# A decode layer's last attention head: four-at-a-time rows of the output projection, another cut of the last V piece, paired output rows

## The chip, the cores and the metric

The kernel runs on one core of one Trainium2 chip. The metric is device time in microseconds (us) of one execution, the median of several. Engines are named as in the profile: PE (TensorE, matrix products), PEld (its weight loads), DVE (VectorE), ACT (ScalarE), POOL (GpSimd) and SP (SyncE, which here only issues transfers). Some transfers can also be issued by ACT.

## The reference

One token passes a layer: layer norm, attention over a cache, projection, residual; then layer norm, a gated feed-forward block, residual.

```
q = (layernorm(x) @ wq)            # 32 query heads of 128, from 512
scores = q . k * 128**-0.5         # 8 key/value heads, 4 query heads share one; 65536 positions
o = softmax(scores) @ v
h = x + o @ wo                     # wo: 4096 x 512
g, u = layernorm(h) @ w_gate, layernorm(h) @ w_up     # 512 x 1792 each
out = h + (sigmoid(g) * u) @ w_down                   # 1792 x 512
```

All inputs are bf16. K and V are 8 x 65536 x 128 each, 268 MB together; with the weights 282 MB are read.

## The kernel before, in words

**Tiles and stages.** The 65536 positions of a head are cut into 32 chunks (`TC` = 16 positions on each of 128 partitions, 512 KB a chunk), and each of K and V comes in two pieces of 16 chunks (`PIECES`), 8 MB each. The pieces go through the buffer `ring`. For each head, DVE transposes K chunk by chunk into `ktw`, PE multiplies by the query (scores into four PSUM banks), the maximum is taken, ACT makes the exponentials, DVE transposes them into `PT_sb`, and PE multiplies V by them (PV). PV goes in *rounds* of two chunks: eight products, on four column groups of the PE array, accumulated in PSUM bank 4 (`PO`). 16 rounds make a head: eight for the first piece, eight for the second.

**What sets the order.** Each engine has its own list of operations; `Prog` puts semaphore waits between them. SP issues all transfers but x in one order (`load`, lines 322 to 360), some behind a wait for a buffer to come free. PE's list for the heads is a loop over code written once, with branches by registers (`pe_flow`, lines 674 to 758). A head has four *parts*, told apart by the register `w`: scores of a quarter of the keys, and in the second and fourth part eight PV rounds of the head before. The eight rounds run as 6 + 2 (registers `m` and `k`), with a detour through `waits` between. A ninth pass of the loop (`i == i_last`) has no scores; it does the PV of head 7 in its second and fourth part, and passes the first and the third empty.

**The last head.** Its second V piece (V7.1) comes as two transfers, 12 chunks and 4 chunks (`LAST`). Ahead of them SP issues w_o as two transfers, the 28 rows that belong to heads 0 to 6 and the last four (`WO`); behind them w_gate, w_up and w_down (`WD_SPLIT`: 8, 4 and 2 of its 14 rows). While V7.1 is under way, PE does section L, which is `project7` and `columns`: `regroup(0)` (L620, L626, L629) puts the outputs of 28 query heads in order in `O3`; 28 products of one column of `O3` with 512 columns of w_o add up one row in PSUM bank 5 (L645, the loop through L430, L663); DVE copies the row to `yr` (L665); four fp32 products turn it into four columns (L671). Then section V3 waits for V7.1's first piece, six PV rounds follow, section VL waits for the second, two rounds follow.

**Behind the last round**: ACT scales and copies the sums (L604), PE adds up and ACT copies them (L607, L610), `regroup(1)` and `project` add the last four query heads (L620, L626, L629, L636, 16 products), layer norm (L807, L388 to L402), gate and up (L821: 32 products of 448 columns, four column groups), the gate's function (L828, L829), the product `hh` (L831), its transpose `hhT` (L834), 56 products with w_down on four column groups, each giving one PSUM row (L839), a copy of four rows of 128 into `y_sb` (L845 on DVE, L847 on ACT, two each), and one transfer out from SP (L849).

L430 is a helper (`mm_at`) through which all products with addresses in registers pass: scores, PV and the w_o rows have that one line.

Of the kernel before, what the change touches and what calls it, by code (L numbers as in the profile page):

```python
# [215 lines left out]
def bass_sequential_preLN__gqa_block_cached__glu_gated_glu__decode_kernel(  # L216
# [18 lines left out]
    RW = 4  # L235
    WD_SPLIT = [(0, 8), (8, 12), (12, 14)]
    FG = FF // 4

    with ExitStack() as es:
        def sb(name, shape, dt):  # L240
            return es.enter_context(nc.sbuf_tensor(name, shape, dt))
# [19 lines left out]
        qz = sb("qz", [128, 8 * 64], bf16)  # L261
        yr = sb("yr", [1, 512], fp32)
        po_sb = sb("po_sb", [128, 512], bf16)
# [29 lines left out]
        hh = sb("hh", [128, FG], bf16)  # L293
        hhT = sb("hhT", [128, FG], bf16)
        y_sb = sb("y_sb", [1, D], bf16)

# [21 lines left out]
        W_AT = {"wg": AT["wg"] * CH, "wu": AT["wg"] * CH + 4 * FF}  # L318
        LAST = [(16, 28), (28, 32)]

# [23 lines left out]
        load("V", h, 0, [f"F{h}.1"], "va", f"V{h}.0")  # L344
        for i, (j0, nj) in enumerate(WO):
            src = A_wo[j0 * DH:(j0 + nj) * DH, :].rearrange("(p r) n -> p (r n)", r=nj)
            dst = ktw[:, j0 * D:(j0 + nj) * D]
            dma("sp", lambda e, src=src, dst=dst: e.dma_start(dst, src), f"wo{i}", [f"PV{h - 1}.3"] if i == 0 else (), f"wo{i}")
        for i, cols in enumerate(LAST):
            load("V", h, 1, (), ("vb", "vl")[i], f"V{h}.1{('', 'b')[i]}", cols)  # L350
        for k, w in (("wg", B_w_gate), ("wu", B_w_up)):
            src = w.rearrange("(p k) n -> p (k n)", p=128)
            for i, (k0, k1) in enumerate(W_SPLIT[k]):
                at = W_AT[k]
                dma("sp", lambda e, at=at, w=src, a=k0 * FF, z=k1 * FF: e.dma_start(ring[:, at + a:at + z], w[:, a:z]),
                    f"{k}{i}", [f"PV{HKV - 1}.1"] if k == "wg" else (), f"{k}.{i}")
# [8 lines left out]
        for nm, t, v in (("onesf", onesf[:, :], 1.0), ("xz0", xz[:, :], 0.0), ("onef", one_f[:, :], 1.0), ("nhalf", nhalf[:, :], -0.5),  # L365
                         ("gs0", gsel[:, :], 0.0), ("zcol", zcol[:, :], 0.0), ("qh0", qh[:, :], 0.0), ("qz0", qz[:, :], 0.0),
                         ("PTz", PT_sb[:, 4 * 512:PT_ROW], 0.0), ("Wz", ktw[:, W0:KTW_ROW], 0.0)):
            op("pool", lambda e, t=t, v=v: e.memset(t, v), name=nm)
# [10 lines left out]
        op("dve", lambda e: e.tensor_reduce(blk_of[:, :], identf[:, :].rearrange("p (c r) -> p c r", r=RW), AX.X, ALU.max), (), "blk")  # L379
        op("dve", lambda e: e.tensor_reduce(bass.AP(tensor=gsel, offset=0, ap=[[128, 128], [32, 4]]),  # L380
                                            identf[:, :].rearrange("p (s j) -> p s j", s=4), AX.X, ALU.add), ["gs0", "identf"], "gsel")

# [87 lines left out]
        op("act", lambda e: e.activation(ps(1, 0, 512, 0, 8), bass.AP(tensor=zcol, offset=0, ap=[[1, 8], [0, 512]]), AF.Copy), ["zcol"], "zq")  # L470
        op("pe", project_q, ["zq", "xz", "wq", "identf", "lsel", "onef", "sel", "gsel", "row", "PTz", "qz0"], "q")
        op("act", lambda e: e.activation(  # L472
# [118 lines left out]
        def pv(h, r, rounds):  # L591
            P.part["pe"] = ("B", (h, r, rounds))
            name = f"PV{h}.{r}" + "a" * (rounds == 6)
            for k in range(2):
# [45 lines left out]
        def project7():  # L640
            regroup(0)
            waits = ["O3.0", "wo0"]
            def rows(e):
                out = ps(YB, 0, D, 0, 1)
                e.matmul(out, lhsT=O3[:, 0:1], rhs=ktw[:, 0:D], start=True, stop=False, skip_group_check=True)  # L645
                ra, ro, rb, rp, left = (reg(e, i) for i in range(16, 21))
                n = NQ - GS
                e.reg_mov(ra, addr_of(ktw, D))
                e.reg_mov(ro, addr_of(O3, 1))
                e.reg_mov(left, n // 2 - 1)  # L650
                e.reg_alu(rb, ra, 2 * D, ALU.add)
                e.reg_alu(rp, ro, 2, ALU.add)
                goto("rows")
                for x, y in ((ra, ro), (rb, rp)):
                    mm_at(e, out, at_reg(O3, y, [[NQ, 128], [1, 1]]), at_reg(ktw, x, [[KTW_ROW, 128], [1, D]]), False, 32)
                for x in (ra, rb):
                    e.reg_alu(x, x, 4 * D, ALU.add)
                for x in (ro, rp):
                    e.reg_alu(x, x, 4, ALU.add)
                e.reg_alu(left, left, -1, ALU.add)  # L660
                e.br_ne(left, 0, on_true="rows", on_false="rows_end")
                label("rows_end")
                return e.matmul(out, lhsT=O3[:, n - 1:n], rhs=ktw[:, (n - 1) * D:n * D], start=False, stop=True, skip_group_check=True)  # L663
            op("pe", rows, waits, "yr")
            op("dve", lambda e: e.tensor_copy(yr[:, :], ps(YB, 0, D, 0, 1)), ["yr"], "yrs")  # L665

        def columns():

            for nt in range(4):
                lhsT = bass.AP(tensor=yr, offset=nt, ap=[[D, 1], [4, 128]])  # L670
                op("pe", lambda e, lhsT=lhsT, nt=nt: e.matmul(ps(YT, nt, nt + 1), lhsT=lhsT, rhs=one_f[0:1, 0:1], start=(nt == 0),  # L671
                                                              stop=False, skip_group_check=True), ["yrs"] if nt == 0 else ())
        def pe_flow(e, section):
# [6 lines left out]

            i, w, p, v, m, k, s = (R.setdefault(n, e.alloc_register(f"r_{n}")) for n in "iwpvmks")
            w0, p0 = addr_of(ktw, W0 + NC - 1 + 127), addr_of(PT_sb, 31 * 4)
# [6 lines left out]
            e.reg_mov(i, i_first)  # L689
            e.reg_mov(s, step[0])  # L690
            goto("head")
            e.reg_mov(w, w0)
# [23 lines left out]
            label("values3")  # L716
            away("br_eq", i, i_last, "rows_of_o", lambda: section("L"))
            e.reg_mov(v, v_at)
# [26 lines left out]
            goto("next", "part")  # L745
            e.reg_alu(w, w, -4, ALU.add)
            e.br_ne(w, w0 - 16, on_true="part", on_false="head_end")
            label("head_end")
            e.br_eq(i, i_last, on_true="after", on_false="more_heads")
            label("more_heads")  # L750
            section("X")
            e.reg_alu(i, i, -lag, ALU.add)
            nc.br("head", engines=here)
            for name, body, back, under in later:
                label(name, under)
                body()
                nc.br(back, engines=here)
            label("after", "head_end")

# [10 lines left out]
        for i in range(HKV + 1):  # L770
            loop, last = 0 < i < HKV, i == HKV
            for r in range(NR):
# [12 lines left out]
                if i and r == 3:  # L785
# [5 lines left out]
                    op("pe", lambda e: None, [f"V{i - 1}.1"])  # L791
                    pv(i - 1, r, 6)
                    if last:
                        P.part["pe"] = ("VL", i)
                        op("pe", lambda e: None, [f"V{i - 1}.1b"])
                    pv(i - 1, r, 2)
                    P.part["pe"] = ("O", i)
# [18 lines left out]
        for i, (nm, bank) in enumerate((("wg", GB), ("wu", UB))):  # L816
            at = W_AT[nm]
            for kt in range(4):
                for c in range(4):
# [13 lines left out]
                                            sg2[:, :].rearrange("p (q r) -> p r q", r=NF), ALU.mult), ["gu1", "sg2"], "hh")  # L833
        op("dve", lambda e: e.transpose(hhT[:, :], hh[:, :]), ["hh"], "hhT")  # L834
        for i, (r0, r1) in enumerate(WD_SPLIT):
            for r in range(r0, r1):
                for g in range(4):
                    last = r == NF - 1 and g == 3
                    op("pe", lambda e, r=r, g=g: e.matmul(  # L839
                        ps(YB, 0, 128, 32 * g, 32 * g + 1), lhsT=hhT[:, 32 * r:32 * r + 1], rhs=wd_v[:, r, g * 128:(g + 1) * 128],  # L840
                        start=False, stop=(r == NF - 1), tile_position=(0, 32 * g), skip_group_check=True),
                       ["hhT", f"wd{i}"] if r == r0 and g == 0 else (), "y" if last else None)
        for g in (0, 2, 1, 3):
            if g < 2:
                op("dve", lambda e, g=g: e.tensor_copy(y_sb[:, 128 * g:128 * g + 128], ps(YB, 0, 128, 32 * g, 32 * g + 1)), ["y"], f"ysb{g}")  # L845
            else:
                op("act", lambda e, g=g: e.activation(y_sb[:, 128 * g:128 * g + 128], ps(YB, 0, 128, 32 * g, 32 * g + 1), AF.Copy),  # L847
                   ["y"], f"ysb{g}")
        dma("sp", lambda e: e.dma_start(out[0], y_sb[:, :]), "out", [f"ysb{g}" for g in range(4)], "out")  # L849
        P.at_end = ("out",)  # L850
        P.emit()
# [28 lines left out]
```

## Time and profile before

| what | value |
|---|---|
| median of 3 runs | 658.86 us (657.86 to 659.07) |
| the profiled execution: own time | 658.92 us |
| its span in the trace | 657.6 us |
| busy: PE / DVE / ACT | 403.7 / 350.7 / 42.9 us |
| read from HBM | 282.33 MB, 429 GB/s over the span |
| mean granted PE clock | 0.78 |
| copy of the output row done, transfer out issued | 656.37, 656.44 us |

How to read it: the profile page shows shares over the whole span; the stages differ, so the end of the kernel is read from the timeline and from the chain of work that ended last. A DMA row gives the time from issue to landing, so a landing is the issue's start plus that time. "issue" in a wait is time in which the engine waited for nothing that the profile shows; on PE it holds register operations and branches. The granted clock is the share of full speed that PE was given.

### The profile page before, as it was taken

What the parts mean: (1) busy time and instruction counts of PE and PEld (TensorE: products, weight loads), DVE (VectorE), ACT (ScalarE), POOL (GpSimd) and SP (SyncE); (2) the same over time, 40 slices, a digit from 0 to 9 for tenths busy, and PEclk for the clock granted to TensorE, in tenths of its full rate; (3) what the DMA queues carried; (4) which work ended last, traced back from release to release, by engine and by line L of the source; (5) the groups of instructions that cost most, each with busy time, mean ns of one, the idle gap of its engine ahead of it and who ended that gap; (6) DMA issues with size and microseconds to landing.
All of it is one profiled execution on the core that took longest, in us unless ns stands there. A gap on an engine that the chain in (4) does not pass through costs nothing. (4 is left out here: it accounts for less than half of the span.)

```text
span 657.6 us, 6197 instructions
## 1 busy us (share of the span) xinstructions
PE 403.7 (61%) x2316; PEld 68.8 (10%) x1548; DVE 350.7 (53%) x427; ACT 42.9 (7%) x114; POOL 3.6 (1%) x17
## 2 busy tenths in 40 slices
PE   2688672938547293764829476382946738285585
PEld 0100010110101010010100101010010101001132
DVE  3398853809266390936628183572908457193102
ACT  1100200020000200001000200002000020002001
POOL 1000000000000000000000000000000000000000
PEclk9889796867959587795958769595786959687677
DMA  9999999999999999999999999999999999999996
GB/s 399 431 440 452 442 419 415 446 446 442 431 403 446 446 446 435 395 446 446 446 435 399 442 446 446 442 407 427 446 446 442 419 415 446 446 442 431 419 410 291
DMA packets 6370, 282.33 MB, mean 429 GB/s; under 512 B 737, under 2 KB 738, under 8 KB 1250
## 3 DMA queue, kind: packets, MB, share of 16 engines
q1 hardware_dynamic: 6338, 282.33, 99.3%
q10 hardware_dynamic: 32, 0.00, 0.0%
HBM read 282.33 MB, written 0.00 MB: 429 GB/s over the span
## 5 line engine op out<-in xcount | busy, mean ns | idle before, releaser
L517 DVE STREAM_TRANSPOSE ktw<-ring 128x1024 f32<-128x1024 f32 x256 | 291.7, 1209 | 165.1 <-DMA ring<-in_A_k_cache_dram 165.1
L430 PE MATMUL PS<-ktw 128*128 128x512 bf16 x1024 | 277.8, 421 | 161.3 <-DVE ktw L517 157.5
L430 PE MATMUL PS<-ring,PT_sb 128*32 x1024 | 87.0, 430 | 51.4 <-issue 47.3
L430 PEld LDWEIGHTS PS<-ktw 128*128 x256 | 26.4, 103 | 401.3 <-issue 236.2
L604 ACT ACTIVATE po_sb<-PS,rl 128x512 bf16<-128x512 f32 x8 | 5.5, 687 | 525.0 <-PE PS L430 525.0
L430 PEld LDWEIGHTS PS<-ring,PT_sb 128*32 x1024 | 20.7, 116 | 115.2 <-issue 113.9
L552 DVE TENSOR_REDUCE gmj<-PS 1x4 f32<-1x128 f32 x8 | 2.2, 278 | 54.5 <-PE PS L550 54.5
L524 DVE TENSOR_REDUCE M_sb<-PS 128x1 f32<-128x512 f32 x32 | 19.9, 682 | 19.3 <-PE PS L430 19.3
L563 ACT ACTIVATE P_sb<-PS,negmax 128x512 bf16<-128x512 f32 x32 | 21.6, 686 | 0.3
L573 DVE STREAM_TRANSPOSE PT_sb<-P_sb 128x512 bf16<-128x512 bf16 x32 | 19.9, 675 | 1.7 <-ACT P_sb L563 1.7
L430 PE MATMUL PS<-ktw,xz 128*8 x32 | 8.8, 443 | 3.6 <-DMA ktw<-in_A_wq_dram 3.6
L620 DVE TENSOR_TENSOR Lw<-O,blk_of 128x896 bf16<-128x896 bf16 (+1 forms) x2 | 1.4, 682 | 13.0 <-ACT O L610 13.0
L550 PE MATMUL PS<-identf,gm 128*1 128x128 f32 x16 | 4.5, 380 | 5.5 <-issue 3.4
L629 DVE CAST O<-PS 128x28 bf16<-128x28 f32 (+1 forms) x2 | 0.3, 173 | 14.0 <-PE PS L626 14.0
L557 PE MATMUL PS<-one_f,gmrep 1*128 1x1 f32 x16 | 4.4, 344 | 5.0 <-DVE gmrep L554 5.0
L430 PE MATMUL PS<-ktw,O 128*1 x26 | 7.0, 433 | 0.0
L475 DVE STREAM_TRANSPOSE qt<-qh 32x512 bf16<-32x512 bf16 x1 | 0.7, 699 | 11.5 <-ACT qh L472 11.5
L563 ACT ACTIVATION_READ_ACCUMULATOR P_sb<-PS,negmax 128x1 f32 x32 | 6.5, 203 | 0.0
L607 PE MATMUL PS<-sel_bf,po_sb 128*128 128x4 bf16 x32 | 2.1, 171 | 6.3 <-ACT po_sb L604 6.3
L490 ACT ACTIVATE PS<-zcol 128x512 f32<-128x512 bf16 x8 | 5.0, 621 | 0.0
L559 ACT ACTIVATE negmax<-PS 128x1 f32<-128x1 f32 x8 | 1.4, 172 | 55.1 <-PE PS L557 55.1
L411 PE MATMUL PS<-xs,xpick 16*128 16x32 bf16 x1 | 0.2, 204 | 7.7 <-DMA xs<-in_A_x_dram 7.7
(88 smaller groups left out, 70.0 us busy)
## 6 DMA issues: line engine op xcount, KB each, us to landing
ring<-in_A_k_cache_dram SPq DMA_DIRECT2D x4, 4096.0 KB, 35.3
ring<-in_A_v_cache_dram SPq DMA_DIRECT2D x1, 6144.0 KB, 32.9
ktw<-in_A_wq_dram SPq DMA_DIRECT2D x1, 4096.0 KB, 12.5
ktw<-in_A_wo_dram SPq DMA_DIRECT2D x1, 3584.0 KB, 18.0
ring<-in_A_v_cache_dram SPq DMA_DIRECT2D x1, 2048.0 KB, 37.3
ring<-in_B_w_gate_dram SPq DMA_DIRECT2D x1, 1792.0 KB, 23.3
ring<-in_B_w_up_dram SPq DMA_DIRECT2D x1, 1344.0 KB, 26.0
ring<-in_B_w_down_dram SPq DMA_DIRECT2D x1, 1024.0 KB, 28.7
```

The costliest lines, as they stand in the source:

```text
L430: return e.add_instruction(mybir.InstMatmult(name=nc.get_next_instruction_name(), engine=mybir.EngineType.PE, ins=[rhs, lhsT], outs=[e.low ...
L490: op("act", lambda e: e.activation(ps(PO, 0, 512), bass.AP(tensor=zcol, offset=0, ap=[[1, 128], [0, 512]]), AF.Copy), ["zcol"] if h == 0 e ...
L517: op("dve", lambda e, d=dst, sr=src: e.transpose(d, sr), deps, f"T{b}.{c}", to="T")
L524: op("dve", lambda e, u=u: e.tensor_reduce(M_sb[:, u % 4:u % 4 + 1], ps(u % NS, 0, 512), AX.X, ALU.max), [f"S{b}.{NC - NR + k}"], f"mx{u}" ...
L550: op("pe", lambda e: e.matmul(ps(MISC, 0, 128, 0, 1), lhsT=gm[:, :], rhs=identf[:, :], start=True, stop=True), [f"gm{h}"], f"gmT{h}", to="Q")
L552: op("dve", lambda e: e.tensor_reduce(gmj[:, :], ps(MISC, 0, 128, 0, 1).rearrange("p (i a c) -> p a i c", a=4, c=NC), AX.XY, ALU.max), [f" ...
L557: op("pe", lambda e: e.matmul(ps(MISC, 128, 129), lhsT=gmrep[0:1, :], rhs=one_f[0:1, 0:1], start=True, stop=True), [f"gmrep{h}"], f"neg{h}")
L559: op("act", lambda e: e.activation(negmax[:, k:k + 1], ps(MISC, 128, 129), AF.Copy, scale=-att_scale), [f"neg{h}"], f"negmax{h}")
L563: op("act", lambda e, b=b: e.activation(P_sb[:, (b % 4) * 512:(b % 4 + 1) * 512], ps(b % NS, 0, 512), AF.Exp, bias=negmax[:, k:k + 1], sca ...
L573: op("dve", lambda e, b=b: e.transpose(PT_sb[:, (b % 4) * 512:(b % 4 + 1) * 512], P_sb[:, (b % 4) * 512:(b % 4 + 1) * 512]), [f"E{b}"], f" ...
L604: op("act", lambda e: e.activation(po_sb[:, :], ps(PO, 0, 512), AF.Copy, scale=rl[:, :]), [f"PV{h}.{NR - 1}", f"rl{h}"], f"po{h}", to="po")
L607: op("pe", lambda e, t=t: e.matmul(ps(OX, 0, 4), lhsT=po_sb[:, t * 128:(t + 1) * 128], rhs=sel_bf[:, 8 * t:8 * t + 8:2], start=(t == 0), s ...
```

## The change

- **w_o rows.** Instead of 28 products into one PSUM row, a loop of seven passes with four products each, on four column groups; each group adds its seven rows in a PSUM row of its own (partitions 0, 32, 64, 96 of bank 5). ACT clears the bank at the start (`zy`). The copy to `yr` takes all 128 partitions, and the four fp32 products of `columns` add up the four rows by a column of `sel_f` that has ones at these partitions.
- **Loop.** In the ninth pass the first and the third part are skipped (step register `d`, entry at `values`), and the code behind the last head follows its last section without a way back through the loop.
- **V7.1** comes as 10 + 6 chunks, so its rounds run as 5 + 3; w_o's last four rows are issued behind it.
- **w_down** comes as 9, 4 and 1 rows.
- **Output.** With padded `hhT` (32 columns, cleared on POOL), two of the four column groups take 32 weight columns of which the last is wanted, so that wanted rows lie side by side at PSUM partitions 31, 32 and 95, 96. DVE and ACT copy 33 partitions each, and two transfers of two rows go out, one from SP and one from ACT. The residual's `gsel` is changed to match.

```
-    WD_SPLIT = [(0, 8), (8, 12), (12, 14)]
+    WD_SPLIT = [(0, 9), (9, 13), (13, 14)]
-        LAST = [(16, 28), (28, 32)]
+        LAST = [(16, 26), (26, 32)]
...
+        load_wo(0, [f"PV{h - 1}.3"])
         for i, cols in enumerate(LAST):
             load("V", h, 1, (), ("vb", "vl")[i], f"V{h}.1{('', 'b')[i]}", cols)
+        load_wo(1, ())
...
+        op("act", lambda e: e.activation(ps(5, 0, 512), bass.AP(tensor=zcol, offset=0, ap=[[1, 128], [0, 512]]), AF.Copy), (), "zy")
...
+                goto("rows")
+                for g in range(4):
+                    mm_at(e, ps(YB, 0, D, 32 * g, 32 * g + 1), at_reg(O3, ys_[g], [[NQ, 128], [1, 1]]),
+                          at_reg(ktw, xs_[g], [[KTW_ROW, 128], [1, D]]), False, 32, 32 * g)
+                for g in range(4):
+                    e.reg_alu(xs_[g], xs_[g], 2 * 4 * D, ALU.add)
+                    e.reg_alu(ys_[g], ys_[g], 2 * 4, ALU.add)
+                e.reg_alu(left, left, -1, ALU.add)
+                e.br_ne(left, 0, on_true="rows", on_false="rows_end")
...
-            op("dve", lambda e: e.tensor_copy(yr[:, :], ps(YB, 0, D, 0, 1)), ["yr"], "yrs")
+            op("dve", lambda e: e.tensor_copy(yr[:, :], ps(YB, 0, D)), ["yr"], "yrs")
...
-            e.br_eq(i, i_last, on_true="after", on_false="more_heads")
-            label("more_heads")
             section("X")
             e.reg_alu(i, i, -lag, ALU.add)
-            nc.br("head", engines=here)
+            e.br_ne(i, i_last, on_true="head", on_false="last_head")
+            label("last_head")
+            e.reg_mov(w, w0 - 4)
+            e.reg_mov(p, p0)
+            e.reg_mov(d, -8)
+            nc.br("values", engines=here)
...
-                    pv(i - 1, r, 6)
+                    pv(i - 1, r, 5 if last else 6)
...
-                    pv(i - 1, r, 2)
+                    pv(i - 1, r, 3 if last else 2)
...
+                    m, c = (1, 32 * r + 32) if g % 2 else (32, 32 * r + 1)
...
+        op("dve", lambda e: e.tensor_copy(y_sb[0:33, :], ps(YB, 0, 128, 0, 33)), ["y"], "ysb0")
+        op("act", lambda e: e.activation(y_sb[64:97, :], ps(YB, 0, 128, 64, 97), AF.Copy), ["y"], "ysb1")
+        for i, eng in enumerate(("sp", "act")):
+            dst = out[0][:, 256 * i:256 * i + 256].rearrange("o (s j) -> (o s) j", s=2)
+            dma(eng, lambda e, i=i, dst=dst: e.dma_start(dst, y_sb[64 * i + 31:64 * i + 33, :]), f"out{i}", [f"ysb{i}"], f"out{i}")
```

## The prediction, on record before the result

> **What bounds the kernel now.** I read the profile page first for the load of the DMA queues, then the landing times, then the chain that ended last, and last the timeline of the final 40 us. From the page, parts 2 and 3 (busy tenths of the DMA engines in 40 slices of 16.4 us; then packets, MB and share of 16 engines' span):
>
> ```profile
> DMA  9999999999999999999999999999999999999996
> ...
> q1 hardware_dynamic: 6338, 282.33, 99.3%
> ```
>
> The transfers run without a hole from the start to the last slice. So nothing that the change does before the last head can move the time, unless it makes the stream stop; the 157.5 us that TensorE (PE) waits for VectorE's transposes cost nothing. What counts is when the last pieces land and what follows them. Part 6 of the page (KB, then us from issue to landing):
>
> ```profile
> ktw<-in_A_wo_dram SPq DMA_DIRECT2D x1, 3584.0 KB, 18.0
> ring<-in_A_v_cache_dram SPq DMA_DIRECT2D x1, 2048.0 KB, 37.3
> ...
> ring<-in_B_w_up_dram SPq DMA_DIRECT2D x1, 1344.0 KB, 26.0
> ring<-in_B_w_down_dram SPq DMA_DIRECT2D x1, 1024.0 KB, 28.7
> ktw<-in_A_wo_dram SPq DMA_DIRECT2D x1, 512.0 KB, 18.9
> ring<-in_B_w_down_dram SPq DMA_DIRECT2D x1, 512.0 KB, 29.5
> ring<-in_B_w_up_dram SPq DMA_DIRECT2D x1, 448.0 KB, 26.7
> ring<-in_B_w_down_dram SPq DMA_DIRECT2D x1, 256.0 KB, 29.6
> ```
>
> Added to the issue times of the timeline (602.0, 602.35, 602.82, 603.3 for w_o and V; 621.64 to 623.9 for the rest) they give the landings: w_o's 28 rows 620.0, its last four 621.25, V7.1's first 12 chunks 635.7 (6144 KB, 32.9 us), its last four 640.6, w_gate 644.9, w_up 648.0 and 649.2, w_down 651.7, 652.9 and 653.5. They land in the order of issue; 13,568 KB in 32.25 us from 621.25 to 653.5 is 431 GB/s, so 512 KB (one chunk of V) is 1.22 us. Now the chain that ended last (start, us, what), its pieces from V7.1 on:
>
> ```profile
> 635.83 0.46 issue
> 636.29 5.58 PE PS L430 x42
> 641.87 1.33 issue
> 643.21 0.63 PE PS L430 x8
> 643.84 0.39 issue
> 644.23 0.66 PE PS L430 x8
> ...
> 649.21 3.19 PE PS L821 x18
> ...
> 654.07 1.69 PE PS L839 x56
> ```
>
> It begins at 635.83, when V7.1's first 12 chunks are there: six rounds of PV, 1.33 us of branches to the last two, and then a row of short steps: 4.33 us from PV's end (644.88) to gate and up (649.21), 1.68 us from their end (652.39) to the w_down product, whose end is at 655.76. At 643.21 the last V piece had been there for 2.6 us, and at 654.07 all of w_down for 0.5 us. So PE's chain is late by a little, and two landings lie close under it: V7.1's pieces ahead, w_down's end behind. A gain can come from an earlier and better cut V7.1, and ends where w_down lands. Last, the timeline of the w_o product before that chain (start, busy us):
>
> ```profile
> 624.07 0.53 PE L626 MATMUL PS<-row_of,Lw 128*128 128x4 bf16 x7 [2.46 <-issue]
> 624.88 0.59 PE L645 MATMUL PS<-ktw,O 128*1 128x512 bf16 x1 [0.28 <-DVE O L629]
> 625.26 6.97 PE L430 MATMUL PS<-ktw,O 128*1 x26
> ...
> 633.22 2.02 PE L671 MATMUL PS<-one_f,yr 1*128 1x1 f32 x8 [0.77 <-DVE yr L665]
> ```
>
> 28 rows of w_o take 7.57 us (624.88 to 632.45), the row's copy 0.68, the turning into columns 2.02; PE is free at 635.24, 0.6 us before V7.1 lands. This stage would be late as soon as V7.1 came earlier; it has to shrink with it.
>
> **The change, part by part.** All times are of the profiled execution: span 657.6, own time 658.92, so 1.32 us lie around the span; the three timed runs have median 658.86, which I treat as the same.
>
> *Order and cut of V7.1.* w_o's last four rows (512 KB) go behind V, and the first piece has 10 chunks instead of 12. It lands 5120 KB behind w_o's 28 rows: 620.0 + 12.15 = 632.1 (before 635.7). The second, 3072 KB, lands 7.3 later: 639.4 (before 640.6). w_o's end lands at 640.7 and is wanted only at 647.03 before, 644.7 after: 4 us of cover. SP issues the same transfers at the same moments, one in another place, none behind a new wait; w_gate still waits for PV7.1 (621.6), with 13 us of transfers queued ahead.
>
> *The w_o rows.* Six branch passings lie between PV7.1's end (621.6) and L626 (624.07), 2.46 us; three are left, so I start the stage 1.2 earlier, with 0 as the other end. Then seven passes of four products on four column groups instead of 28 products. A PV round has eight products and some 19 register operations in 0.97 to 1.02 us, at half clock and at full clock alike; a pass here has half of both, so 0.5 us, 3.5 in all. Ends: 3.0 (512 columns at half clock, 0.43) and 6.9 (a whole round's 0.98 each). Copy and columns stay 0.68 and 2.02: the copy's partitions go from 1 to 128, its 512 columns stay. The stage ends at 622.9 + 0.8 + 3.5 + 0.1 + 0.8 + 2.0 = 630.1, under V7.1's 632.1.
>
> *PV of the last quarter.* The first round is 0.46 behind the landing as now, at 632.6; five rounds need 4.9 (636.29 to 641.2 before): 637.5; the branches of 1.33 end at 638.8, under the second landing at 639.4, with 0.6 to spare. Then 0.46 and three rounds (2 x 1.02 + 0.66 = 2.70): PV ends at 642.56 instead of 644.88, **2.32 earlier**. This is the heart of the forecast: three rounds instead of two behind the last landing, but that landing decides.
>
> *Gate, up and w_down.* With the 4.33 us of steps, L821 starts at 646.89 and ends at 650.08; w_up is there at 648.0 and 649.2, wanted at 648.5 and 649.7, so not late. The product with w_down could start at 651.76, but its first piece, now nine rows, lands at 652.0: **w_down's landings are what is late next**. 36 products at 1.69/56 = 0.030 end at 653.14; four rows land at 653.2 and take 0.48, to 653.73; the last row, landed at 653.5, takes 0.12: 653.85, which is 1.91 earlier than 655.76. Half of these products have weights of 32 columns instead of one. No row has that with 128 columns moving: below, nothing (PV's 32-column loads lie beside its products); above, 28 times the 0.024 of one load (1.37 us for 56), 0.7. I take 0.15, since only the products behind the last landing can show it in full.
>
> *The output.* Four copies, two on each engine one after the other (655.78 to 656.37), become one on each: 0.28 as each of them now, 33 partitions instead of 1, so 0.31 less. Two transfers of two rows go out from SP and ACT instead of one from SP. SP's took 0.32 to issue and 0.8 to land; ACT's only issue in the trace took 0.38: 0.05 more.
>
> *The start.* One clear of a PSUM bank on ACT (0.6, as the one at 2.64) and one small memset on POOL (0.1): the projection waits for w_q until 13.2, and both engines are through by 4. Nothing.
>
> Sum: -1.91 + 0.15 - 0.31 + 0.05 = -2.0 us: 658.92 - 2.0 = **656.9**. With all costs at nothing and PE never late, w_down's landing (653.5), one row (0.12 + 0.05) and the shorter output leave 656.6: the floor.
>
> **The rivals.** *Half clock in the tail.* By the granted clock in stretches of half a us, PE's clock is full from 641.3 to 648.2 and half from 634.5 to 641.3 and after 648.2. After the change PE stands idle from 637.5 to 639.9, so the last rounds and the steps behind may run at half. The last round would take 0.94 instead of 0.66 (the round at 620.66 did); L636's 16 products 16 x 0.076 (L626: seven in 0.53 at half clock) = 1.2 instead of 0.7. L821 ends at 650.86, w_down's product starts at 652.54 and ends with the 0.15 at 654.38: -1.38 - 0.26 = -1.64, **657.3**. The Trainium skill, "TensorE: Matmul & The Clock Gate", section on the HAM clock gate, has the clock judged in free-running windows of about 3.4 us, so that it would differ from run to run; the trace's changes, at 617.45, 620.85, 627.68, 634.51, 641.33 and 648.17, all one or two times 3.4 apart, agree. By that rule half clock in the tail is neither sure nor excluded.
>
> *The rows do not run side by side.* If four column groups with one row each go one after another, the stage takes its 7.57 again: it ends at 634.1, PV starts at 635.1, five rounds, branches and three rounds end at 644.05: -0.83. w_down's product then starts at 653.24 and ends at 655.08: -0.68 - 0.26 = -0.94, **658.0**, no measurable change. For it: no row here has four one-row products side by side. Against it: L821 does just that with 448 columns, 32 in 3.15 us at half clock, 0.37 for four.
>
> *ACT's queue is slow to write out*, the case on the other side. The only transfer from ACT in the trace, x, took 6.9 us from issue to landing, SP's output about 1.1. If the second pair of rows needs x's time, the end is 654.3 + 6.9 = 661.3 of span, +3.7: **662.6**, slower; it decides from 3.2 us on. Against it: x was issued together with 4 MB of w_q, the output into an idle queue. The Trainium skill, "DMA: Bandwidth & Descriptors", section "Issuing engines are not separate DMA queues", has all issuing engines share the same 16 DMA engines, which speaks for SP's time here; no run shown has ACT write out.
>
> **How the numbers follow.** Forecast 0.54 and floor 0.06, both faster; half clock 0.22, of which two thirds end beyond 0.2% and one third within; rows in series 0.10, within; ACT's queue, or a stop of PE that I do not see, 0.08, slower. 0.2% is 1.32 us, about what a measurement of this kernel can tell from no change (the runs shown lie from 657.86 to 659.07). So faster 0.75, same 0.17, slower 0.08. The range goes from 656.2 (the floor, less 0.4 for the spread of runs) to 658.0 (rows in series).
>
> **What would show it.** Right: V7.1's pieces land near 632 and 639.4; the w_o stage is done before 632; PE waits for V ahead of the last three rounds; PV ends near 642.6; the w_down product waits for a landing and ends near 654. Wrong: the stage ends after 632.7 (rows), 16 products of L636 take 1.2 (clock), a last transfer that ends over 2 us behind its copy (queue), or the last landing is later than 653.5: small last pieces cost the stream time, and each 0.1 there is 0.1 at the end.

## The result, and the profile after

The changed kernel takes 656.57 us (median of 7, 656.31 to 656.72) against 658.85 (median of 7): ratio 0.9967, 95% interval 0.9956 to 0.9978. The forecast was 656.9. The profiled execution took 656.72 with a span of 655.4, so 1.32 us lie around the span as before, and the span is 2.2 shorter.

The page's DMA row of the changed kernel (busy tenths in 40 slices) never falls under 80%, now up to the last slice. Below it stand the transfers that give the landings (KB, us from issue to landing):

```profile
DMA  9999999999999999998999999999999989999998
```

```profile
ktw<-in_A_wo_dram SPq DMA_DIRECT2D x1, 3584.0 KB, 18.3
ring<-in_A_v_cache_dram SPq DMA_DIRECT2D x1, 3072.0 KB, 36.8
...
ring<-in_B_w_down_dram SPq DMA_DIRECT2D x1, 1152.0 KB, 29.6
ktw<-in_A_wo_dram SPq DMA_DIRECT2D x1, 512.0 KB, 37.6
ring<-in_B_w_down_dram SPq DMA_DIRECT2D x1, 512.0 KB, 30.3
```

V7.1's ten chunks (5120 KB, issued at 602.03, 30.0 us) land at 632.0 and the six at 602.5 + 36.8 = 639.3; w_o's end lands at 640.6; w_down's pieces land at 651.9 (issued at 622.33) and 653.1. The timeline of PE in the changed kernel (start, busy us; in brackets the idle time before and what ended it):

```profile
622.47 0.54 PE L631 MATMUL PS<-row_of,Lw 128*128 128x4 bf16 x7 [1.51 <-issue]
623.67 3.89 PE L434 MATMUL PS<-ktw,O 128*1 x28 [0.66 <-DVE O L634]
...
628.36 2.03 PE L675 MATMUL PS<-sel_f,yr 128*128 128x1 f32 x8 [0.80 <-DVE yr L669]
632.57 4.74 PE L434 MATMUL PS<-ring,PT_sb 128*32 x40 [2.18 <-PEq L171]
639.92 0.77 PE L434 MATMUL PS<-ring,PT_sb 128*32 x8 [2.61 <-DMA ring<-in_A_v_cache_dram]
640.90 2.05 PE L434 MATMUL PS<-ring,PT_sb 128*32 x16 [0.21 <-issue]
...
647.22 3.16 PE L838 MATMUL PS<-ring,hc 128*1 128x448 bf16 x32 [0.25 <-DVE hc L825]
...
652.07 0.68 PE L857 MATMUL PS<-ring,hhT 128*32 128x128 bf16 x36 [1.19 <-DVE hhT L851]
653.19 0.53 PE L857 MATMUL PS<-ring,hhT 128*32 128x128 bf16 x20 [0.43 <-DMA ring<-in_B_w_down_dram]
```

Three things are to be seen. The 28 rows of w_o take 3.89 us instead of 7.57, and the stage ends at 630.39, 1.6 us before V lands. Between the last quarter's five and three rounds PE stands idle for 2.61 us and is released by the transfer of V: the second landing sets the chain, as forecast. And the w_down product, cut in two by a wait of 0.43 us, is now held by w_down's second piece. It ends at 653.75 instead of 655.76. The chain of work that ended last says the same (start, us, what): it now runs through that transfer, where in the kernel before it held only the work of the engines from 635.83 on.

```profile
622.80 30.34 DMA ring<-in_B_w_down_dram
653.15 0.04 issue
653.19 0.56 PE PS L857 x17
```

### The profile page after: what moved, and what is told of

The parts are those of the page before. It is cut to its first block, busy times and chain, and to the rows that moved or that the text cites. A ratio compares the mean times of both kernels' runs of the same rounds, so it can differ in the third digit from the quotient of the medians.

```text
span 655.4 us, 6173 instructions
## 1 busy us (share of the span) xinstructions
PE 397.5 (61%) x2317; PEld 66.0 (10%) x1549; DVE 350.5 (53%) x426; ACT 43.1 (7%) x114; POOL 3.6 (1%) x18
## 4 chain that ended last, share of the span: by engine, by line
DMA 66%; DVE 31%; PE 1%; issue 1%; SPq 0%; PEldq 0%
DMA ring<-in_A_k_cache_dram 58%; DVE ktw L522 31%; DMA ring<-in_B_w_down_dram 5%; DMA ring<-in_A_v_cache_dram 4%; PE PS L434 1%; SPq L359 0%; PE PS L857 0%; SPq L364 0%; SPq L330 0%; DVE y_sb L861 0%; PEldq L171 0%
## 5 line engine op out<-in xcount | busy, mean ns | idle before, releaser
L583 PE MATMUL PS<-L_sb,lsel 128*128 128x4 f32 x16 | 2.5, 229 | 3.8 <-DVE PT_sb L578 3.8
## 6 DMA issues: line engine op xcount, KB each, us to landing
ring<-in_A_v_cache_dram SPq DMA_DIRECT2D x1, 3072.0 KB, 36.8
```

The costliest lines, as they stand in the source:

```text
L583: op("pe", lambda e: e.matmul(ps(MISC, 132, 136), lhsT=lsel[:, :], rhs=L_sb[:, :], start=True, stop=True), [f"PT{NR * h + NR - 1}"], f"l{h ...
```

## The experiments

Each time is a median, beside the ratio to the kernel before on the same chip with its interval. The intervals are some 0.1% to either side, 0.7 us; smaller differences between two variants are read from the traces, which show one execution each. The variants ran on two chips (e1 to e4 on one, e5 to e12 on the other); the kernel before had medians of 658.86 on the one and 658.81 and 658.78 on the other, 658.85 beside the changed kernel, so medians are set side by side as they are. All runs are also listed with their span: own time less span is 1.3 us in most, but 2 to 2.8 in some runs, most of them of e12 and of the kernel before. Where that matters I give the median span beside it (changed kernel: 655.2).

**One part alone, on the kernel before.** e1 has the order and the cut, e2 the rows and the loop:

```
 e1    LAST = [(16, 26), (26, 32)]; rounds 5 + 3; load_wo(1) behind V7.1
 e2    rows four at a time, loop without empty parts; the rest as before
```

> The kernel before with V7.1 cut 10 + 6 (rounds 5 + 3) and w_o's last four rows behind V; rows, loop, w_down's pieces and output as before. My theory: the w_o stage still ends at about 635.2, so PV of the last quarter starts at 635.7 instead of 636.3 though its first piece lands at 632; five rounds, 1.33 us of branches and three rounds end at 644.7 to 645.0 against 644.9: no change, 658.8 (658.4 to 659.2). Rival, the earlier landings alone carry the gain: PV ends at 642.6 and the time is 656.9 to 657.2.

Measured: 657.02, ratio 0.9978 (0.9968 to 0.9988). By the median my theory of no change fell. But the times lie in two groups, eight from 656.68 to 657.20 and four from 658.58 to 658.86, and the profile came from the later one (658.85). In that profile PV ends at 644.8, as the theory has it, but by another way: the stage ends only at 636.5, and the five rounds then take 3.97 us, not 4.9.

> The kernel before with the w_o rows four at a time and the shorter loop, all else (order, cut, w_down's pieces, output) as before. My theory: the stage ends near 630.5, but PV waits for V7.1's first 12 chunks until 635.7, so it starts at 636.2 as before: no change, 658.7 (658.4 to 659.0). Rival, the shorter stage carries the gain: 657 or less.

Measured: 658.55, 0.9995 (0.9987 to 1.0004): no change, as expected. The trace shows where the shorter stage went: the columns are done at 630.6, and the first PV round starts at 636.49, 5.84 us later, as late as before:

```profile
628.62 2.03 PE L675 MATMUL PS<-sel_f,yr 128*128 128x1 f32 x8 [0.80 <-DVE yr L669]
636.49 5.63 PE L434 MATMUL PS<-ring,PT_sb 128*32 x48 [5.84 <-PEq L171]
```

To see what e1 gains from, e9 and e10 split it, and e11 runs it again:

```
 e9    load_wo(1) behind V7.1; LAST = [(16, 28), (28, 32)]
 e10   LAST = [(16, 26), (26, 32)]; rounds 5 + 3; w_o ahead of V7.1
```

> The kernel before with one thing changed: w_o's last four rows are issued behind V7.1. Theory as mended by the first runs: V7.1's first 12 chunks land at 634.5, before the w_o stage ends (635.2 to 636.5, by PE's clock); PE has then already issued the rounds and starts them right behind the stage, without the 1.05 us gap of before; six rounds and branches end near 641.6 and PV at 643.3 to 643.8: 1.1 to 1.6 faster, 657.3 to 657.8. By the theory of the prediction (a gap and 0.97 a round again) it would be 658.6 or more.

Measured: 657.68, 0.9986 (0.9977 to 0.9995). The median is 1.1 us lower, about half of the whole gain, and all that was changed is one transfer of 512 KB, issued 1 us later. The chain of e9 (start, us, what):

```profile
633.89 2.02 PE PS L675 x8
635.91 3.37 PE PS L434 x16
...
640.91 1.34 issue
642.25 0.99 PE PS L434 x8
643.27 1.07 PE PS L434 x8
...
653.54 0.98 PE PS L843 x56
```

The columns end at 635.91, and PV begins at 635.91. V had landed at 634.8, and what cost 1.05 us before (the branches and register operations ahead of the first round) has passed while the columns were still being computed. That is what my expectation for e1 had left out. The prediction leaves it out in the rival of serial rows too: it counts a gap and 4.9 us for five rounds, where e1 shows no gap and 3.97.

The last line matters as well. In this profile PV ends at 644.35, 0.53 us earlier than in the kernel before, and yet the product with w_down ends 1.2 us earlier: its 56 products take 0.98 us at full clock, where they took 1.69 at half clock. So over half of what this profile gains comes from the clock in the tail. How the clock stood there in the other runs of e9 was not seen; so what the order alone is worth, between the 0.5 of this trace and the 1.1 of the median, stays open.

> The kernel before with the cut alone: 10 + 6 chunks, rounds 5 + 3, order as before. The first piece lands at 633.3, before the stage ends, the second at 640.6 as before. Five rounds right behind the stage end at 639.3, PE waits until 641.1, three rounds end at 643.8 to 644.0: 657.9 (657.6 to 658.3). If order and cut add up to the 1.8 of both together, this and the order alone share it; if each alone gives nearly all, they overlap.

Measured: 657.91, 0.9992 (0.9983 to 1.0001); in the profile (657.70) the five rounds end before the second landing at 640.67, and PV ends at 644.35, again 0.53 earlier than in the kernel before, and again the product with w_down takes 0.98 at full clock. By medians, order (-1.1) and cut (-0.9) alone add up to about the -1.8 of e1; by the ratios it is 0.9 and 0.5 against 1.4. With the clock in play and intervals of 0.6 us this does not show that the two add up.

> The kernel of the first run (order and cut only) once more, since its times fell in two groups (656.7 to 657.2 and 658.6 to 658.9) and its profile came from the later group. Theory: in the earlier group more of the w_o rows ran at full clock, so the stage ended at 635.3 or earlier, and PV by 643.3. In a profile of about 657 the rows take under 7.6 us; in one of about 658.8 again 8.5. If a profile of about 657 shows the rows at 8.5, the two groups come from something else.

Measured: 658.35, 0.9986 (0.9975 to 0.9998); three of eight runs from 656.99 to 657.19, five from 658.25 to 659.09, and again a profile of a late one (659.09): its rows take 8.6 us. With e1 that is 11 early runs and 9 late ones of 20. How long the serial rows take follows the granted clock: it rose to full at 627.7 in the kernel before (rows 7.57 us), at 628.7 in e9 (7.95), at 629.9 in e1 (8.5), at 630.2 in e11 (8.6). In the late runs the stage so ends at 636.5 to 636.7 and hides the early landing. Whether the early runs had full clock from the first row on was not seen, since no profile of one came up; that stays open. The stage can hardly be all of the 1.8 us between the groups: in both late profiles the product with w_down ran at half clock too (1.69), and full clock there, as in e9 and e10, would be 0.7 of it.

**One part undone, on the changed kernel.** In e3 the rows go one after another, in e4 and e7 the cut is another, in e12 the order is the old one:

```
 e3    mm_at(e, ps(YB, 0, D, 0, 1), ..., False, 32, 0)        # all in column group 0
 e4    LAST = [(16, 28), (28, 32)]; rounds 6 + 2
 e7    LAST = [(16, 24), (24, 32)]; rounds 4 + 4
 e12   load_wo(1) ahead of V7.1
```

> The changed kernel with the same row loop, but all four products of a pass in column group 0, so that they run one after another. My theory: the stage takes its 7.6 us again and ends at 634.1; PV starts at 634.6, its five rounds and the branches end at 640.7 instead of waiting for the landing at 639.3; PV ends 0.8 later, of which some 0.2 to 0.4 vanishes in the wait for w_down: 657.2 (657.0 to 657.4). If the stage were hidden whatever it takes: 656.6. If column groups bring nothing beside each other, the loop takes the same 3.9 as in the changed kernel.

Measured: 656.81, 0.9972 (0.9960 to 0.9983). The column groups do work beside each other: in series the rows take 8.3 us (623.44 to 631.74, from 627.7 on at full clock), four at a time 3.9, all at half clock. Yet it costs only 0.24 by the medians, less than two such medians can tell apart:

```profile
632.53 2.03 PE L675 MATMUL PS<-sel_f,yr 128*128 128x1 f32 x8 [0.79 <-DVE yr L669]
634.49 4.03 PE L434 MATMUL PS<-ring,PT_sb 128*32 x40
639.67 0.63 PE L434 MATMUL PS<-ring,PT_sb 128*32 x8 [1.15 <-DMA ring<-in_A_v_cache_dram]
...
651.78 1.87 PE L857 MATMUL PS<-ring,hhT 128*32 128x128 bf16 x56 [1.38 <-DMA ring<-in_B_w_down_dram]
```

PV starts 1.9 us later than in the changed kernel, but without a gap, and five rounds take 4.03 instead of 4.74: they are through before the second landing. The last line shows the floor: here PV ended 0.7 us earlier than in the changed kernel (642.28 against 642.95), the w_down product then waits for w_down's *first* piece, takes 1.9 us at half clock, and ends at 653.68 against 653.75. What is gained ahead of w_down is taken back there.

> The changed kernel with V7.1 cut 12 + 4 again (rounds 6 + 2). My theory: the first piece lands at 634.4, six rounds and the branches end at 642.0, 2.7 us behind the second landing; PV ends at 643.8 instead of 643.0, and after the wait for w_down 0.5 to 0.7 of it is left: 657.2 (657.0 to 657.3). If the cut matters nothing because w_down's landing decides: 656.6.

Measured: 656.74, 0.9975 (0.9963 to 0.9987), one of six runs at 658.3. Less than I expected: in the profile the branches behind the sixth round took 0.89 instead of 1.33, and PV ended at 643.26, 0.3 behind the changed kernel's. The w_down product then waited for no transfer.

> The changed kernel with V7.1 cut 8 + 8 (rounds 4 + 4). My theory: PV starts at 630.9, right behind the w_o stage, and waits from 636 for the second landing at 639.3; four rounds of 1.0 follow instead of three: PV ends 1.0 later, of which 0.6 to 0.8 is left behind the wait for w_down: 657.2 (657.1 to 657.5). With the 12 + 4 cut it makes a curve with its low at 10 + 6.

Measured: 657.30, 0.9976 (0.9967 to 0.9986), span 655.9, as expected: four rounds behind the second landing (639.84 to 643.9). By their medians 12 + 4, 10 + 6 and 8 + 8 give 656.74, 656.57 and 657.30; the first two are not told apart.

> The changed kernel with w_o's last rows ahead of V7.1 again. My theory: both pieces of V land 1.2 later, at 633.3 and 640.5, PE waits for both, PV ends at 643.9 to 644.2 instead of 643.0, and the wait for w_down takes 0.4 of it up: 657.2 (656.9 to 657.5). If the landings of V no longer matter because w_down's sets the end: 656.6.

Measured: 657.82, 0.9993 (0.9983 to 1.0003), span 656.4. The direction is right, the size is not: 1.2 of span instead of 0.6. In the profile, the shortest run (657.11), the two landings came at 633.1 and 640.3 and PV ended at 644.04, as expected, and the w_down product no longer waits. Five of the twelve runs lie from 659.1 to 659.5, partly by time outside the span (2.1 to 2.8). What made the rest of the spans longer is not settled. In the profile the 56 products took 1.00 us at full clock; half clock there would add 0.7, but no profile of a longer run shows it.

**The end.** e5 has the output as before, e6 both transfers from SP, e8 leaves 448 KB out of the stream:

```
 e5    hhT without padding, four copies of one row, one transfer
 e6    for i, eng in enumerate(("sp", "sp")):
 e8    w_up's last quarter not loaded
```

> The changed kernel with the output as before: weights of one column, four copies of one row, one transfer from SP. My theory: the copies cost 0.29 more, the single transfer 0.10 to 0.15 less: 656.7 (656.6 to 656.9). If two transfers from two engines cost as much as the copies save: 656.57 or less.

Measured: 656.96, 0.9971 (0.9958 to 0.9983), 0.39 above the changed kernel, just over the 0.33 that the expectation allowed; in the traces the copies end 0.29 apart (654.35 against 654.06) and the spans 0.2 (655.6 against 655.4).

> The changed kernel with both output transfers issued by SP, one behind the other. My theory: the second is issued 0.35 to 0.45 behind the first, ACT's issue took 0.50 against SP's 0.33, so the end comes 0.2 to 0.3 later: 656.8. Rival, ACT's queue is the slow one: 656.57 or less.

Measured: 656.84, 0.9969 (0.9957 to 0.9981), 0.27 above by the medians, 0.2 by the spans of the two profiles. ACT's queue is not slow. Its issue is the longer one, but two issues on SP take 0.64 in a row. The output of the changed kernel:

```profile
654.08 0.50 ACTq L865 DMA_DIRECT2D out_dram<-y_sb  x1
654.09 0.33 SPq L865 DMA_DIRECT2D out_dram<-y_sb  x1
```

> The changed kernel without the load of w_up's last quarter (448 KB): the products run with what is left in the buffer, so the output is not the layer's. All of w_down lands 1.05 us earlier, V7.1 as before. My theory: PE waits 0.43 us for w_down's second piece now; that wait goes, and then PE's own chain sets the end: 656.57 - 0.4 = 656.15 (656.0 to 656.3). If the stream alone sets the end: 655.5. If PE's chain alone does: 656.57.

Measured: 657.01, 0.9964 (0.9950 to 0.9978), outside the range expected; five runs from 655.68 to 657.48, their median span 655.2, the same as the changed kernel's. So 1.05 us less of stream behind V brings nothing that these runs can tell. In the profile the wait for w_down is gone, but the 56 products run at half clock and take 1.68 us:

```profile
651.85 1.68 PE L859 MATMUL PS<-ring,hhT 128*32 128x128 bf16 x56 [0.98 <-DVE hhT L853]
```

They end at 653.57, 0.2 earlier than in the changed kernel and 1.5 behind the last landing (652.1), so in this run the stream does not set the end.

The profiles of e5 and e6, which have all the loads, bear on this too. There the product starts right behind `hhT` (651.91, 651.89), runs at half clock with a wait of 0.2 and 0.3 us for w_down in it, and ends at 653.74 and 653.78; the changed kernel's profile has full clock, a wait of 0.43, and 653.75. So at half clock the loads of w_down hold the product up by some 0.2 us, and that is all that e8 could bring there. What it would bring at full clock was not seen in a profile; its shortest run, with a span of 654.4, would fit a larger gain. The wait for w_down and PE's own chain lie within a few tenths of each other, and the clock that PE has in the product decides by how much.

## Why the prediction was right, step by step

- **Landings.** 632.1 and 639.4 were predicted, 632.0 and 639.3 measured. The sum by bytes at 431 GB/s held to 0.1 us.
- **The w_o stage.** Predicted to start at 622.9 and end at 630.1; measured 622.47 and 630.39. A pass of four took 0.53 us (predicted 0.5). That the end is so close is in part luck: the steps took 7.9 us instead of 7.2 (1.20 instead of 0.8 up to the first row, 3.89 instead of 3.6 for the rows), and the earlier start hid 0.4 of it.
- **PV.** First round at 632.6 predicted, 632.57 measured; second wait over at 639.9, measured 639.92. The chain that ended last begins with the transfer of this second piece in e5, e6, e8, e10 and e12 too. The three rounds were mis-sized: 3.03 us instead of 2.70; the clock fell to half at 640.3, and the last round took 1.05. PV ended at 642.95 instead of 642.56.
- **What is late next.** w_down's landing, as predicted, though its second piece (653.1) and not its first: with PV 0.4 later, PE came to the product at 652.07, 0.1 behind the first landing. The product ended at 653.75; predicted was 653.85, or 654.0 with the loads of 32 columns. The step holds in other profiles too: the product waits for the first piece in e3, and for 0.2 and 0.3 us in e5 and e6.
- **Loads of 32 columns.** 0.15 was taken, 0.02 at most is measured. At half clock 56 products without a wait took 1.68 us in e8, 1.66 with one-column weights before; at full clock 0.96 in e7 and e12, 0.95 with one-column weights in e9 and e10.
- **Output.** Copies 0.31 less, as predicted. From the copies' end to the end of the span it is 1.34 us instead of 1.23, so 0.1 more instead of 0.05.

For the profiled run the forecast is 0.2 too late (656.9 against 656.72): 0.25 in the product, of which 0.15 for loads that cost nothing and 0.1 because the second piece landed 0.1 earlier and the clock was full, less the 0.05 of the output. The median of the seven runs lies another 0.15 lower.

**The half-clock rival** came true in its cause and in a part of its price. The clock was half from 640.3 to 650.5. The last rounds cost 0.33 us more, near the 0.28 that it has for them, but L641's 16 products took 0.69 us as before, where they had run at full clock. Windows of the changed kernel and of the kernel before (stretch, length, PE busy with count, granted clock, DMA share, GB/s):

```profile
645.00:646.00 1.00, 0.69 (x16) 0.50 0.98 419
```

```profile
647.00:647.50 0.50, 0.47 (x14) 1.00 0.92 373
647.50:648.00 0.50, 0.22 (x7) 1.00 0.96 394
```

The 1.2 us had been scaled from L626's seven products, 0.53 us at half clock; in the changed kernel they take 0.54 at full clock. Neither group took longer at half clock. The Trainium skill, "TensorE: Matmul & The Clock Gate", section on the HAM clock gate, has free-running windows of 3.4 us; the changes in the changed kernel, at 616.4, 623.2, 636.9, 640.3, 650.5 and 653.9, are again whole multiples of 3.41 apart (2, 4, 1, 3 and 1), so this trace agrees.

**The rival of serial rows** was mispriced: 658.0 predicted, 656.81 in e3. The price had PE begin the rounds anew behind the stage, with a gap and some 0.98 us a round; with the data there, no gap is seen (e3, e7, e9), and in e3 five rounds took 4.03.

**The slower rival** (ACT's queue) is refuted by the changed kernel itself, whose span ends 1.34 us behind the copies, and by e6: with SP alone it is later, not earlier. The Trainium skill's "DMA: Bandwidth & Descriptors", section "Issuing engines are not separate DMA queues", allows a second issuing engine only the saved issue time; e6 shows 0.27 us beside an issue of 0.31, so the run agrees.

**Where the 2.3 us come from.** Order and cut alone bring some 1.8 of them in 11 of 20 runs and next to nothing in the other 9 (e1, e11); by the ratios of the two sets it is 1.4 and 0.9. Undoing the order alone costs 1.25 (e12). The output brings 0.2 by the traces, 0.4 by the medians. Rows and loop alone bring nothing (e2), but with order and cut they take most of the spread out of the end: 9 of 20 runs without them ended past 658.2; none of the 6 runs of e5, which adds them and the w_down pieces, ended past 657.5, and none of the changed kernel's 7 past 656.8. Of the two the loop may do most of that, since with the rows in series (e3) none of 6 runs ended past 657.6. Neither the loop nor w_down's new pieces (9, 4, 1) were tried alone.

## What to carry to other kernels

Where the transfers never stop, write down the landing of each of the last pieces and the moment when its user is ready: the gain of reordering 512 KB is at most that landing's shift, and ends at the next landing that is late. A step that ends just before a landing is worth shortening only together with an earlier landing, and then also because its own spread over runs stops showing. When two bounds at the end lie within half a us, taking one away can bring nothing (e8). And where the granted clock differs from run to run, look at it in both profiles before putting a gain down to the change: in e9 it was 0.7 of 1.2 us.

## What the runs showed of the hardware

- The register operations and branches of a PE loop were partly hidden where earlier products still ran and the data was there: PV began right at the end of the columns in e9 (635.91) and five rounds took 3.97 to 4.1 us (e1, e3, e9, e10, e11), against 4.6 to 5.0 where PE had waited for the data (the changed kernel, e5, e6, e12), and a gap of 1.05 us ahead of them in the kernel before. In e7 the data landed only some 0.7 us before the columns ended (an estimate: 4096 KB at 431 GB/s behind w_o's 28 rows, at 619.8); there the gap was gone, but four rounds took 3.87. That the sequencer issues ahead is the reading that fits; it was not measured by itself.
- Four one-row products of 512 columns on four column groups took 0.53 us together at half clock; one after another they took 0.43 each at half clock.
- Products of one column with a full set of weights took the same time at half and at full clock: 16 in 0.69 us. Products of 128 columns did not: 56 took 0.95 us at full clock (e9, e10) and 1.66 at half (the kernel before, e1).
